# Window attention and a SoLU layer on one core: where two of four loads stand, what a load is planned at, and two transposes set apart

## The chip, the core and the metric

The kernel runs on one core of one Trainium2 chip. The metric is device time in microseconds of one execution. The core's engines are TensorE (PE in the profile; PEld is its weight load), VectorE (DVE), ScalarE (ACT) and GpSimd (POOL); SyncE (SP) issues the DMAs and computes nothing. Each engine works through its own instructions in the order in which the program holds them and waits for the others by semaphores.

## The reference

Eight batches of eight heads attend over 576 positions, each position to itself and the 63 before it; the result is a 4608 x 512 matrix, which goes through a layer with a SoLU activation and a layer norm.

```
scores = where(0 <= rel < 64, q @ k.T / 8, -1e9)
attn   = softmax(scores);  x = attn @ v             # to 4608 x 512
h      = x @ w_in                                   # 512 -> 1024
solu   = h * softmax(h)
ln     = (solu - mean) / sqrt(var + 1e-6) * g_ln
out    = ln @ w_out                                 # 1024 -> 512
```

## The kernel before, in words

**Tiles.** The 4608 tokens are 36 tiles of 128. For each tile the stages are, with the lines of the profile:

- *load* (L338, L343): one DMA brings the tile's queries and keys (qk, 640 KB), one its values (v, 512 KB). Each has a ring of three buffers.
- *scores* (L373, PE), *softmax*: mask and maximum on VectorE (L388), exponential on ScalarE (L393), sums and reciprocals on VectorE (L406, L409), then eight scalings by the reciprocal, one for each head, on GpSimd (L411).
- *cross*: from tile 5 on the softmax tile is turned by DMA. ScalarE copies it, as two halves of 16-bit planes, into a buffer called raw (L425), and SyncE issues one DMA transpose for each half (L428).
- *transposes*: VectorE copies the turned planes into PT (L435). Tiles before the fifth are turned on PE (L446) and copied by ScalarE or VectorE (L451).
- *values* (L470, PE), whose result is split by ScalarE (L484) and VectorE (L485) into a high part xH and a low part xL.
- *moe_in* (L513): 24 matmuls of 512 columns, in three passes (high by high, high by low, low by high), into the only buffer pH. The first three tiles do it in plain fp32 (L502).
- *moe_norm*: maximum on VectorE (L528), exponential on ScalarE (L530), the product with h on VectorE (L533), which is the last to read pH; the sum of squares on ScalarE (L539), small steps for the factor kk on VectorE (L536 to L547) with a power on GpSimd between them (L546), and on GpSimd two halves of the final scaling of e (L550).
- *moe_cross*: VectorE copies each half of e to planes (L576) and SyncE issues a DMA transpose for each (L579); *moe_join* copies the turned planes back into y (VectorE, L589) and splits them (ScalarE L593, VectorE L595). The last two tiles are turned on PE instead, in *moe_transpose* (L610), where ScalarE takes the high part (L619) and VectorE the low one (L621); tiles 0 to 2 go that way as well (L615 for the first two).
- *moe_out* (L646): 24 matmuls, then a copy (ScalarE, L653) and a store (SyncE, L654).

**Order.** At tile t the program runs moe_in of t, the normalisation of t, and moe_out of t - 2. From tile 6 on the attention work is done in pairs: `group(t)`, at every second tile, holds the values of t+1 and t+2, the scores of t+3 and t+4, the loads, and the softmax and cross of t+3 and t+4.

The program doesn't issue instructions directly. It builds a list (`Plan`): each entry has an engine, a cost in nanoseconds, what it reads and writes, and a delay until others may use the result. PE keeps the order of the list. For the others a planner runs the list as in a timetable, by those costs: among the entries of an engine that could begin it takes the one that is due first, counted back from PE's order. SyncE's entries are in the order of the list for the first tiles; those marked loose (loads, stores and transposes of tiles after the third) may be placed freely. A DMA's cost is its size divided by 340 bytes per nanosecond, at least 350 ns. So a change of a cost or of a place in the list can move instructions on SP, DVE, ACT and POOL, and none on PE.

Tensors in the planned orders have the tile's number behind their name (e_18, qk_27). In raw the buffers count 8 for the weights, then 2t + 8 for tile t's softmax planes and 2t + 9 for its planes of the MoE part: raw_54 is the softmax of tile 23, raw_51 the MoE part of tile 21.

Of the kernel before, what the change touches and what calls it, by code (L numbers as in the profile page):

```python
# [18 lines left out]
P = 128  # L19
# [7 lines left out]
AHEAD = 3  # L27
# [15 lines left out]
PAIRS = 6  # L43

SPL = 3

# [8 lines left out]
class Plan:  # L57
# [12 lines left out]
        self.ops.append((engine, cost, emit, reads, writes, lat + self.LATENCY, loose))  # L70

    def dma(self, size, emit, reads, writes, loose=False):
        self.op("SP", max(350, size // 340), emit, reads, writes, 2600, loose)

    def edges(self):

# [91 lines left out]
def tile_window_attention_solu_moe(  # L168
# [17 lines left out]
    nc = tc.nc  # L186

    NT, DM = out.shape
# [6 lines left out]
    NF = DFF // P  # L195
    NTILE = NT // P
    NW = NC + NF // 2
# [23 lines left out]
    for first in (0, None, 1):  # L221
        t = masks[first] = const.tile([P, P], F32, name=f"mask{first}")
# [11 lines left out]
    plan = Plan(RINGS)  # L234

    def T(tag, n, shape, dtype=F32, pool=None):

        if (tag, n) not in plan.tiles:
            plan.tiles[tag, n] = (pool or sb).tile(
                shape, dtype, tag=tag, name=f"{tag}_{n}", bufs=RINGS[tag])  # L240
        return plan.tiles[tag, n]
# [8 lines left out]
    def W32(i):  # L250
        return T("w", i, [P, 2, 512])

    def WL(i):
        return T("w", NW + i, [P, 2, 512], F32R)

    def WH(i, x):
        if i < NC:
            return w_inH[:, i, x * 512:(x + 1) * 512]
        return w_outH[:, 2 * (i - NC) + x]
# [63 lines left out]
    def QK(t):  # L323
        return T("qk", t, [P, NPAIR * (2 * P + WIN)])
# [7 lines left out]
    def V(t, half):  # L332
        return T("v", t, [P, 2, DM])[:, half]

    def load(t, parts=range(2)):

        if 0 in parts:
            plan.dma(P * P * 40, lambda: nc.sync.dma_start(QK(t), qk[t]), [], [("qk", t)],  # L338
                     t > SPL)


        if 1 in parts:
            plan.dma(P * P * 32, lambda: nc.sync.dma_start(  # L343
                T("v", t, [P, 2, DM]).rearrange("p a n -> p (a n)"), v[t]), [], [("v", t)], t > SPL)

    def SS(t):
        return T("sS", t, [P, H, P])
# [7 lines left out]
    def PE_T(t, x):  # L355
        return PS(NTILE + t)[:, x]
# [61 lines left out]
    def XP(t):  # L418
        return T("raw", NW + 2 * t, [P, 4, 2, 512], U16)

    def cross(t):
        if t < CROSS_P:
            return
        for x in range(2):
            plan.op("ACT", 1050, lambda x=x: nc.scalar.copy(  # L425
                XP(t)[:, x], SS(t)[:, 4 * x:4 * x + 4].bitcast(U16).rearrange("p h (n w) -> p w (h n)", w=2)),
                [("sS", t, 4 * x + i) for i in range(4)], [("raw", NW + 2 * t, x)])
            plan.op("SP", 1250, lambda x=x: nc.sync.dma_start_transpose(  # L428
                XP(t)[:, 2 + x].rearrange("p w (h n) -> p (w h) n", h=4), XP(t)[:, x].rearrange("p w n -> p (w n)")),
                [("raw", NW + 2 * t, x)], [("raw", NW + 2 * t, 2 + x)], 2600, t > SPL)  # L430

# [61 lines left out]
    def E(t):  # L493
        return T("e", t, [P, DFF])
# [59 lines left out]
    def YH(t):  # L554
        return T("yH", t, [P, NF, P], F32 if t < PLAIN_OUT else F32R)

    def YL(t):
        return T("yL", t, [P, NF, P], F32R)

    def crosses(t):  # L560
        return CROSS_FROM <= t < NTILE - CROSS_END
# [4 lines left out]
    def EP(t, h):  # L566
        return XB(t)[:, h]

    def TP(t, h):
        return XB(t)[:, 2 + h].rearrange("p w (f n) -> p w f n", f=4)  # L570

    def moe_cross(t):
        if not crosses(t):
            return
        for h in range(2):
# [4 lines left out]
                TP(t, h).rearrange("p w f n -> p (w f) n"), EP(t, h).rearrange("p w n -> p (w n)")),  # L580
                [("raw", NW + 2 * t + 1, h)], [("raw", NW + 2 * t + 1, 2 + h)], 2600, t > SPL)

    def moe_join(t):
        def Y(h):
            return T("y", t, [P, NF, P])[:, 4 * h:4 * h + 4]

        for h in range(2):
            hs = slice(4 * h, 4 * h + 4)
            plan.op("DVE", 740, lambda h=h: nc.vector.tensor_copy(  # L589
                Y(h).bitcast(U16).rearrange("p f (n w) -> p f w n", w=2),  # L590
                TP(t, h).rearrange("p w f n -> p f w n")),
                [("raw", NW + 2 * t + 1, 2 + h)], [("y", t, h)])
            plan.op("ACT", 620, lambda h=h, hs=hs: nc.scalar.copy(YH(t)[:, hs], Y(h)),  # L593
                    [("y", t, h)], [("yH", t, h)])
            plan.op("DVE", 620, lambda h=h, hs=hs: nc.vector.tensor_sub(  # L595
                YL(t)[:, hs], Y(h), YH(t)[:, hs].bitcast(F32)),
                [("y", t, h), ("yH", t, h)], [("yL", t, h)])

    def moe_transpose(t):
        if crosses(t):  # L600
            moe_join(t)
            return
        for h in range(2):
            def pT(h=h):
                return PE_T(t, h)

            def emit(h=h, pT=pT):
                for f in range(4):
                    c = 4 * h + f
                    nc.tensor.transpose(pT()[:, f], E(t)[:, c * P:(c + 1) * P], ident)  # L610

            hs = slice(4 * h, 4 * h + 4)
            plan.op("PE", 430, emit, [("e", t, h)], [("pS", NTILE + t, h)])
            if t < PLAIN_OUT:
                plan.op("DVE", 620, lambda hs=hs, pT=pT: nc.vector.tensor_tensor(  # L615
                    YH(t)[:, hs], pT(), g_sb[:, hs].unsqueeze(2).to_broadcast([P, 4, P]), op=ALU.mult),
                    [("pS", NTILE + t, h), ("g",)], [("yH", t, h)])
                continue
            plan.op("ACT", 560, lambda hs=hs, pT=pT: nc.scalar.copy(YH(t)[:, hs], pT()),  # L619
                    [("pS", NTILE + t, h)], [("yH", t, h)])  # L620
            plan.op("DVE", 620, lambda hs=hs, pT=pT: nc.vector.tensor_sub(  # L621
                YL(t)[:, hs], pT(), YH(t)[:, hs].bitcast(F32)),
                [("pS", NTILE + t, h), ("yH", t, h)], [("yL", t, h)])

    def moe_out(t, middle=None):

        tag = ("pO", t)

        def PO():
            return T(*tag, [P, DM], pool=ps_o)  # L630

        if t < PLAIN_OUT:
            for f in range(NF):
                plan.op("PE", 860, lambda f=f: nc.tensor.matmul(  # L634
                    PO(), YH(t)[:, f], W32(NC + f // 2)[:, f % 2],
                    start=(f == 0), stop=(f == NF - 1)),
                    [("yH", t, f // 4), ("w", NC + f // 2), ("w", NC + f // 2, f % 2)], [tag])
        for f in range(NF if t >= PLAIN_OUT else 0):
            if f == NF // 2 and middle is not None:
                moe_transpose(middle)  # L640
            i, x = NC + f // 2, f % 2
            for k, (y, w, keys) in enumerate((
                    (YH, lambda i, x: WH(i, x), [("yH", t, f // 4), ("H", i, x)]),
                    (YH, lambda i, x: WL(i)[:, x], [("yH", t, f // 4), ("w", NW + i, x)]),
                    (YL, lambda i, x: WH(i, x), [("yL", t, f // 4), ("H", i, x)]))):
                plan.op("PE", 233, lambda f=f, i=i, x=x, k=k, y=y, w=w: nc.tensor.matmul(  # L646
                    PO(), y(t)[:, f], w(i, x), start=(f == k == 0), stop=(f == NF - 1 and k == 2)),
                    keys, [tag])

        def ot():  # L650
            return T("ot", t, [P, DM])

        plan.op("ACT", 580, lambda: nc.scalar.copy(ot(), PO()), [tag], [("ot", t)])  # L653
        plan.dma(P * DM * 4, lambda: nc.sync.dma_start(out[t * P:(t + 1) * P, :], ot()), [("ot", t)], [],  # L654
                 t > SPL)

    def on(f, t, *args):
        if 0 <= t < NTILE:
            f(t, *args)


    def attend(t):
        on(scores, t + AHEAD)
        on(softmax, t + AHEAD)
        on(cross, t + AHEAD)

    load(0, range(1))
    prep(0)
    scores(0)
    softmax(0)  # L670
    load(0, range(1, 2))
    prep(1)
    prep(2)
    load(1)
    transposes(0)
    values(0)
# [10 lines left out]
    def group(t):  # L687
        on(values, t + 1)
        if t != PAIRS:
            on(values, t + 2)  # L690
        both = t + AHEAD, t + AHEAD + 1
        for u in both:
            on(scores, u)
        for u in (t + AHEAD + 2, t + AHEAD + 3):
            on(load, u, range(1))
        for u in (t + AHEAD + 1, t + AHEAD + 2):
            if u != PAIRS + AHEAD + 2:
                on(load, u, range(1, 2))
        for u in both:
            on(softmax, u)  # L700
            on(cross, u)

    for t in range(NTILE + BEHIND):
        if t < PAIRS:
# [17 lines left out]
        else:  # L722
# [22 lines left out]

            last = NTILE - 1 <= t < NTILE + BEHIND - 1
            on(moe_out, t - BEHIND, *([t - BEHIND + 1] if last else []))

    order = plan.order()
# [46 lines left out]
```

## Time and profile before

| | us |
| --- | --- |
| three runs of the kernel | 535.96, 534.41, 532.65 (median 534.41) |
| the profiled execution | 536.71 |
| its span in the trace | 534.9 |

| busy in the span | us | share |
| --- | --- | --- |
| PE, matmuls | 508.7 | 95% |
| PEld, weight loads | 394.4 | 74% |
| DVE | 419.2 | 78% |
| ACT | 357.2 | 67% |
| POOL | 221.6 | 41% |

The profile is of one execution. Busy times are sums over instructions; an engine that is idle is mostly waiting for another, and only what PE waits for can lengthen the execution directly. A wait is put down to the semaphore that came last. The chain of waits is followed back from the last instruction. The granted clock is TensorE's: 1.00 is full speed.

### The profile page before, as it was taken

Reading aid. Unit: us, or ns where it says so; the run is one execution under the profiler, and the core shown is the slowest. Engines: PE = TensorE matmul, PEld = TensorE weight load, DVE = VectorE, ACT = ScalarE, POOL = GpSimd, SP = SyncE. Lnnn points to the kernel's source line nnn. Section 1 sums busy time; section 2 is a strip of 40 time slices with the busy share of each in tenths; the row PEclk is TensorE's granted clock in tenths of the full one; section 3 lists DMA queues with packets and bytes.
Section 4 is the critical chain, followed back from the end, with each engine's and each line's share of the span. In section 5 each row is a group of like instructions: output and inputs, shape, how many; then the busy total and the mean of one; then the engine's idle time right before and its main releaser. Section 6 shows DMA issues by size and latency. Waiting matters only on the chain.

```text
span 534.9 us, 11673 instructions
## 1 busy us (share of the span) xinstructions
PE 508.7 (95%) x4072; PEld 394.4 (74%) x4072; DVE 419.2 (78%) x1327; ACT 357.2 (67%) x959; POOL 221.6 (41%) x406
## 2 busy tenths in 40 slices
PE   2779999999999999999999999979999999999996
PEld 2345576778888887787878787868887888788775
DVE  4979997988787978797979697778777879698630
ACT  4587866679677767677768677684857694956331
POOL 2046067243616461626362526272617161615220
PEclk9989999999999999999999999999999999999999
DMA  8994225789978887777888887967778878457301
GB/s 321 410 387 142 88 74 88 197 191 233 179 217 158 220 155 218 157 217 159 217 158 217 158 217 157 213 132 199 165 156 204 157 215 174 91 104 111 80 21 40
DMA packets 148508, 93.58 MB, mean 175 GB/s; under 512 B 132960, under 2 KB 132960, under 8 KB 148064
## 3 DMA queue, kind: packets, MB, share of 16 engines
q1 hardware_dynamic: 148448, 92.83, 71.0%
q8 instruction: 32, 0.52, 0.4%
q14 instruction: 28, 0.23, 0.1%
HBM read 50.86 MB, written 9.44 MB: 113 GB/s over the span
## 4 chain that ended last, share of the span: by engine, by line
PE 65%; DVE 11%; POOL 8%; DMA 8%; ACT 5%; issue 2%; ACTq 0%; POOLq 0%; DVEq 0%
PE pO L646 26%; PE pH L513 24%; DMA raw<-raw 7%; POOL sS L411 6%; PE pO L470 4%; PE pS L373 4%; PE pH L502 4%; POOL e L550 2%; ACT sS L393 2%; DVE sS L388 1%; DVE raw L576 1%; PE pO L634 1%; DVE PT L435 1%; DVE mst L528 1%; DVE y L589 1%
## 5 line engine op out<-in xcount | busy, mean ns | idle before, releaser
L411 POOL TENSOR_SCALAR sS<-sS,rec 128x128 f32<-128x128 f32 x280 | 122.0, 456 | 49.6 <-DVE nmx L388 26.7
L393 ACT ACTIVATE sS<-sS,nmx 128x128 f32<-128x128 f32 x288 | 111.8, 391 | 10.4 <-DVE nmx L388 9.9
L546 POOL TENSOR_TENSOR mst<-mst,neghalf 128x1 f32<-128x1 f32 x36 | 30.2, 840 | 203.7 <-DVE mst L544 203.7
L646 PE MATMUL pO<-w_outH,yH 128*128 128x512 f32 x272 | 110.1, 405 | 1.2 <-DVE xL L485 1.1
L513 PE MATMUL pH<-w_inH,xH 128*128 128x512 f32 x264 | 106.8, 405 | 3.5 <-DVE mst L533 3.0
L646 PE MATMUL pO<-w,yH 128*128 128x512 f32 x272 | 108.1, 398 | 0.0
L646 PE MATMUL pO<-w_outH,yL 128*128 128x512 f32 x272 | 106.9, 393 | 0.1
L513 PE MATMUL pH<-w,xH 128*128 128x512 f32 x264 | 104.9, 401 | 0.0
L513 PE MATMUL pH<-w_inH,xL 128*128 128x512 f32 x264 | 104.1, 394 | 0.0
L550 POOL TENSOR_SCALAR e<-e,mst 128x512 f32<-128x512 f32 x72 | 66.4, 928 | 45.1 <-DVE mst L547 20.4
L425 ACT COPY raw<-sS 128x1024 uint16<-128x1024 uint16 x62 | 64.3, 1045 | 30.7 <-POOL sS L411 30.6
L589 DVE COPY y<-raw 128x1024 uint16<-128x1024 uint16 x62 | 48.7, 785 | 24.0 <-DMA raw<-raw 23.9
L539 ACT ACTIVATE sq<-e,mst 128x1024 bf16<-128x1024 f32 x36 | 41.4, 1149 | 36.3 <-DVE mst L536 25.0
L513 PEld LDWEIGHTS pH<-w_inH,xH 128*128 128x128 f32 x264 | 49.9, 189 | 18.8 <-issue 3.2
L646 PEld LDWEIGHTS pO<-w_outH,yH 128*128 128x128 f32 x272 | 51.0, 187 | 16.6 <-DVE xL L485 2.4
L576 DVE COPY raw<-e 128x1024 uint16<-128x1024 uint16 x62 | 47.7, 775 | 17.2 <-POOL e L550 17.2
L646 PEld LDWEIGHTS pO<-w_outH,yL 128*128 128x128 f32 x272 | 51.1, 188 | 13.2 <-DVE yL L621 0.5
L513 PEld LDWEIGHTS pH<-w_inH,xL 128*128 128x128 f32 x264 | 50.1, 190 | 12.7 <-issue 0.2
L646 PEld LDWEIGHTS pO<-w,yH 128*128 128x128 f32 x272 | 51.1, 188 | 10.9
L513 PEld LDWEIGHTS pH<-w,xH 128*128 128x128 f32 x264 | 49.9, 189 | 11.4 <-issue 0.2
L388 DVE CUSTOM_DVE_ANT_0 sS<-pS,maskNone 128x128 f32<-128x128 f32 x224 | 53.0, 283 | 4.2 <-PE pS L373 4.2
L593 ACT CAST yH<-y 128x512 fp32r<-128x512 f32 x62 | 38.1, 616 | 26.8 <-DVE y L589 12.5
(66 smaller groups left out, 751.5 us busy)
## 6 DMA issues: line engine op xcount, KB each, us to landing
qk<-qk SPq DMA_DIRECT2D x36, 640.0 KB, 5.6
v<-vS SPq DMA_DIRECT2D x36, 512.0 KB, 4.8
y<-ot SPq DMA_DIRECT2D x36, 256.0 KB, 2.5
raw<-w_out SPq DMA_DIRECT2D x4, 1024.0 KB, 10.8
raw<-w_in SPq DMA_DIRECT2D x3, 1024.0 KB, 11.5
raw<-raw SPq DMA_TRANSPOSE x124, 3.3
raw<-w_in SPq DMA_DIRECT2D x2, 512.0 KB, 6.3
g_sb<-gT SPq DMA_DIRECT2D x1, 4.0 KB, 14.4
```

Source lines behind the costliest of these rows:

```text
L388: plan.op("DVE", 215, lambda h=h: nc.vector.tensor_tensor_reduce(SS(t)[:, h], PS(t)[:, h % 2, h // 2], mk, scale=-SCALE, scalar=BIG, op0=A ...
L393: plan.op("ACT", 390, lambda h=h: nc.scalar.activation(SS(t)[:, h], SS(t)[:, h], AF.Exp, bias=cols("nmx", h), scale=-1.0, accum_out=cols(" ...
L411: plan.op(engine, cost, lambda h=h: v.tensor_scalar(SS(t)[:, h], SS(t)[:, h], rec()[:, h:h + 1], 0.0, ALU.mult, ALU.add), [R], [("sS", t, h)])
L425: plan.op("ACT", 1050, lambda x=x: nc.scalar.copy(XP(t)[:, x], SS(t)[:, 4 * x:4 * x + 4].bitcast(U16).rearrange("p h (n w) -> p w (h n)", ...
L513: plan.op("PE", 233, lambda n=n, c=c, x=x, w=w: nc.tensor.matmul(PH(t)[:, hs], x(t)[:, c], WH(c, h) if w is WH else WL(c)[:, h], start=(n ...
L539: plan.op("ACT", 1200, lambda: nc.scalar.activation(T("sq", t, [P, DFF], BF16), E(t), AF.Square, bias=nmean(), scale=1.0, accum_out=ss()), ...
L546: plan.op("POOL", 560, lambda: nc.gpsimd.tensor_tensor(kk(), kk(), neghalf, op=ALU.pow), [], [key(5)])
L550: plan.op("POOL", 770, lambda h=h, hs=hs: nc.gpsimd.tensor_scalar(E(t)[:, hs], E(t)[:, hs], nmean(), kk(), ALU.add, ALU.mult), [key(4), ke ...
L576: plan.op("DVE", 740, lambda h=h: nc.vector.tensor_copy(EP(t, h), E(t)[:, h * 512:(h + 1) * 512].bitcast(U16).rearrange("p (n w) -> p w n" ...
L589: plan.op("DVE", 740, lambda h=h: nc.vector.tensor_copy(Y(h).bitcast(U16).rearrange("p f (n w) -> p f w n", w=2), TP(t, h).rearrange("p w ...
L593: plan.op("ACT", 620, lambda h=h, hs=hs: nc.scalar.copy(YH(t)[:, hs], Y(h)), [("y", t, h)], [("yH", t, h)])
L646: plan.op("PE", 233, lambda f=f, i=i, x=x, k=k, y=y, w=w: nc.tensor.matmul(PO(), y(t)[:, f], w(i, x), start=(f == k == 0), stop=(f == NF - ...
```

## The change

The planner now takes the loose loads and stores at 240 bytes per nanosecond instead of 340. This is a number of the planner alone; on the chip the transfers have the same size and form. In `group`, the qk load of the even tile (t+6) and the v load of t+4 stay where they were; the qk load of the odd tile (t+7) and the v load of t+5 are listed after softmax and cross and read a key, "gate", which the two plane copies of tile t+4 write. So they are planned behind these copies. The key stands for no data: the loads get no semaphore from it, only their place in SyncE's order. Third, in the two last moe_outs, which hold the transposes of the next tile in their middle, the second half of these transposes comes two rows of w_out, that is six matmuls, later than the first.

```diff
@@ Plan.dma
-        self.op("SP", max(350, size // 340), emit, reads, writes, 2600, loose)
+        self.op("SP", max(350, size // (RATE if loose else 340)), emit, reads, writes, 2600, loose)
@@ load(t, parts=range(2), after=())   # both DMAs: reads [] becomes list(after)
@@ cross
-                [("sS", t, 4 * x + i) for i in range(4)], [("raw", NW + 2 * t, x)])
+                [("sS", t, 4 * x + i) for i in range(4)], [("raw", NW + 2 * t, x), ("gate", t)])
@@ moe_transpose(t, halves=range(2))
-        for h in range(2):
+        for h in halves:
@@ moe_out
-            if f == NF // 2 and middle is not None:
-                moe_transpose(middle)
+            if f in (NF // 2, NF // 4 * 3) and middle is not None:
+                moe_transpose(middle, (f // 2 % 2,))
@@ group
-        for u in (t + AHEAD + 2, t + AHEAD + 3):
-            on(load, u, range(1))
-        for u in (t + AHEAD + 1, t + AHEAD + 2):
-            if u != PAIRS + AHEAD + 2:
-                on(load, u, range(1, 2))
+        if t == PAIRS:
+            on(load, t + AHEAD + 2, range(1))
+        on(load, t + AHEAD + 3, range(1))
+        on(load, t + AHEAD + 1, range(1, 2))
         for u in both:
             on(softmax, u)
             on(cross, u)
+        on(load, t + AHEAD + 4, range(1), [("gate", t + AHEAD + 1)])
+        if t != PAIRS:
+            on(load, t + AHEAD + 2, range(1, 2), [("gate", t + AHEAD + 1)])
```

RATE is 240 and AHEAD is 3. In the changed file the lines stand one or two further down. The instructions are the same in number and kind; on PE only the last transposes move. Three places, each before and then after:

SyncE, from the loads of tiles 26 to 29 to the transposes of tile 22's MoE planes, first before:

```order
L343 DMA v_26_3930<-vS 128x1024
L343 DMA v_27_3956<-vS 128x1024
L338 DMA qk_28_3990<-qk 128x1280
L579 DMA_TRANSPOSE raw_51_3994<-raw_51_3994 128x8x128 x2
L338 DMA qk_29_4035<-qk 128x1280
L579 DMA_TRANSPOSE raw_53_4087<-raw_53_4087 128x8x128 x2
```

Three loads precede the transposes of tile 21 (raw_51), and a fourth those of tile 22. Now SyncE has, from tile 24's softmax planes (raw_56) on:

```order
L430 DMA_TRANSPOSE raw_56_3824<-raw_56_3824 128x8x128 x2
L344 DMA v_25_3865<-vS 128x1024
L656 DMA y<-ot_19_3854 128x512
L339 DMA qk_27_3890<-qk 128x1280
L344 DMA v_26_3940<-vS 128x1024
L581 DMA_TRANSPOSE raw_51_3936<-raw_51_3936 128x8x128 x2
L339 DMA qk_28_4012<-qk 128x1280
L581 DMA_TRANSPOSE raw_53_4084<-raw_53_4084 128x8x128 x2
```

The odd tiles' v and qk have moved up behind the softmax planes, into the group before, on either side of a store; v_26 alone still stands just ahead of raw_51, and qk_28 between the two pairs. All later groups look alike.

GpSimd, from the power of tile 18 (L546) to the scalings of tile 19's e, first before:

```order
L546 TENSOR_TENSOR mst_18_3262<-mst_18_3262,neghalf_100 128x1
L550 TENSOR_SCALAR e_18_3288<-e_18_3288,mst_18_3262 128x512
L411 TENSOR_SCALAR sS_21_3322<-sS_21_3322,rec_21_3428 128x128 x8
L411 TENSOR_SCALAR sS_22_3376<-sS_22_3376,rec_22_3457 128x128 x8
L550 TENSOR_SCALAR e_18_3288<-e_18_3288,mst_18_3262 128x512
L546 TENSOR_TENSOR mst_19_3471<-mst_19_3471,neghalf_100 128x1
L550 TENSOR_SCALAR e_19_3485<-e_19_3485,mst_19_3471 128x512 x2
```

The sixteen softmax scalings of tiles 21 and 22 stand between the two halves of tile 18's e. Now:

```order
L548 TENSOR_TENSOR mst_18_3262<-mst_18_3262,neghalf_100 128x1
L552 TENSOR_SCALAR e_18_3286<-e_18_3286,mst_18_3262 128x512 x2
L413 TENSOR_SCALAR sS_21_3321<-sS_21_3321,rec_21_3425 128x128 x8
L413 TENSOR_SCALAR sS_22_3367<-sS_22_3367,rec_22_3454 128x128 x8
L548 TENSOR_TENSOR mst_19_3468<-mst_19_3468,neghalf_100 128x1
L552 TENSOR_SCALAR e_19_3485<-e_19_3485,mst_19_3468 128x512 x2
```

Both halves precede the sixteen. The same holds now for tiles 10, 16, 18 and so on to 30; before it held for tiles 16 and 22 alone of those with softmax scalings behind them, and tile 26 had eight scalings between its halves.

VectorE in the start, around the first reduction of tile 2 (mst_2), with the copy of tile 3's PT and the low part of a weight (w_8), first before:

```order
L312 TENSOR_TENSOR w_8_588<-w_0_145,w_inH_97 128x512
L451 COPY PT_3_547<-pS_75_539 128x512
L615 TENSOR_TENSOR yH_0_602<-pS_36_591,g_sb_99 128x512
L528 TENSOR_REDUCE mst_2_621<-pH_2_550 128x1
L293 SCALAR_TENSOR_TENSOR w_7_534<-raw_7_422,w_7_534 128x1024
```

Now:

```order
L292 TENSOR_SCALAR w_7_552<-w_7_552 128x1024
L296 SCALAR_TENSOR_TENSOR w_6_458<-raw_6_399,w_6_458 128x1024
L530 TENSOR_REDUCE mst_2_587<-pH_2_550 128x1
L453 COPY PT_3_548<-pS_75_536 128x512
L617 TENSOR_TENSOR yH_0_604<-pS_36_589,g_sb_99 128x512
L294 SCALAR_TENSOR_TENSOR w_7_552<-raw_7_451,w_7_552 128x1024
```

The reduction has moved ahead of the copy of PT_3 and of tile 0's yH.

More of the change, by code (lines that the diff above doesn't have):

```diff
@@ L45 @@
 SPL = 3
+RATE = 240
 RINGS = {
@@ L333, in V, with load @@
         return T("v", t, [P, 2, DM])[:, half]
-    def load(t, parts=range(2)):
+    def load(t, parts=range(2), after=()):
         if 0 in parts:
-            plan.dma(P * P * 40, lambda: nc.sync.dma_start(QK(t), qk[t]), [], [("qk", t)],
+            plan.dma(P * P * 40, lambda: nc.sync.dma_start(QK(t), qk[t]), list(after), [("qk", t)],
                      t > SPL)
@@ L343, in load @@
             plan.dma(P * P * 32, lambda: nc.sync.dma_start(
-                T("v", t, [P, 2, DM]).rearrange("p a n -> p (a n)"), v[t]), [], [("v", t)], t > SPL)
+                T("v", t, [P, 2, DM]).rearrange("p a n -> p (a n)"), v[t]), list(after), [("v", t)],
+                t > SPL)
     def SS(t):
@@ L597, in moe_join, with moe_transpose @@
                 [("y", t, h), ("yH", t, h)], [("yL", t, h)])
-    def moe_transpose(t):
+    def moe_transpose(t, halves=range(2)):
         if crosses(t):
```

## Prediction

> **What bounds the kernel now.** I first read the span, then the busy times by stretch (weights and ramp, 0 to 50; the steady part, 95 to 505; the tail, from 505), to see where TensorE stands idle.
>
> ```profile
> span 534.9 us, 11673 instructions
> 0.00:50.00 50.00, 33.72 (x317) 19.45 (x318) 36.99 (x136) 30.94 (x93) 15.77 (x44) 0.97 0.82 317
> ...
> 95.00:505.00 410.00, 405.01 (x3315) 326.67 (x3314) 333.74 (x1072) 285.03 (x765) 179.83 (x323) 1.00 0.78 176
> 505.00:534.90 29.90, 25.13 (x115) 19.74 (x113) 7.88 (x17) 7.97 (x14) 4.75 (x6) 1.00 0.10 36
> ```
>
> The columns are the stretch, its length, the busy time of PE, PEld, DVE, ACT and POOL, the granted clock, the DMA share and GB/s. PE is busy for 405.01 of 410 us in the steady part, so everything the change could win there is the other 4.99 us, plus whatever a low clock costs. The first stretch has 16.28 us without PE, which belong to weight preparation, and the tail 4.77. The matmuls themselves stay. Next come the waits that end PE's idle time, in the steady part (two rows) and in the tail (one):
>
> ```profile
> PE pH L513 <- DVE mst L533: 3.0, 2, 2.8
> PE pO L646 <- DVE xL L485: 1.1, 2, 0.9
> PE pS L610 <- ACT yH L619: 1.1, 1, 1.1
> ```
>
> One wait of 2.8 us makes most of it: a moe_in that waits until VectorE's product (L533) has read the single pH buffer. The chain of waits shows what was late (start, length, what):
>
> ```profile
> 317.29 5.63 PE pH L513 x24
> ...
> 338.94 0.63 DVE raw L576 x2
> 339.57 6.41 DMA raw<-raw
> ...
> 346.01 0.76 DVE y L589
> 346.77 0.04 DVE mst L547
> ...
> 346.98 2.58 POOL e L550 x2
> 349.55 4.78 POOL sS L411 x8
> ...
> 354.35 0.03 ACT raw L425
> ...
> 355.31 1.21 ACT e L530 x2
> ...
> 356.54 1.23 DVE e L533
> ...
> 357.92 7.36 PE pH L513 x24
> ```
>
> Two DMA transposes of tile 21's normalised planes take 6.41 us. On VectorE the copy of their result (L589) stands ahead of L547, which tile 22's scalings on GpSimd need; behind those stand the softmax scalings, then ScalarE's copies to the planes, behind one of them tile 23's exponential, then its product, then PE. The last row holds a second loss: 24 matmuls took 7.36 us where 24 took 5.63 at 317.29, so 1.73 more. The same columns for the 3.4 us behind the stall show a clock of 0.63 there:
>
> ```profile
> 357.90:361.30 3.40, 3.38 (x10) 2.69 (x11) 3.23 (x10) 3.14 (x6) 0.11 (x1) 0.63 0.67 124
> ```
>
> The stall thus costs 2.78 + 1.73 = 4.51 us.
>
> **The change part by part. Later loads.** SyncE's own sequence at that place, and the landing times of the MoE transposes (minimum, median, maximum) issued in three windows, 338 to 342, 255 to 262 and 421 to 425:
>
> ```profile
> 335.29 1.52 SPq L343 DMA_DIRECT2D v<-vS  x2
> 337.27 0.33 SPq L338 DMA_DIRECT2D qk<-qk  x1
> 339.57 3.87 SPq L579 DMA_TRANSPOSE raw<-raw  x2
> ```
> ```profile
> DMA to landing us min/median/max: 6.4/6.6/6.8
> DMA to landing us min/median/max: 4.3/4.4/4.5
> DMA to landing us min/median/max: 3.5/3.6/3.7
> ```
>
> In the first two windows two v loads and a qk load stand just ahead of the pair; in the third only one v load does. The new order puts one load, the even tile's v, there, and places the odd tile's v and qk behind the four softmax-plane transposes. So I cost the odd tile's MoE transposes as in the third window: 6.6 - 3.6 = 3.0 us earlier at the worst place.
>
> What 3.0 us do to the stall is shown by the place 83 us earlier (tile 17), where GpSimd and VectorE have the same order as at tile 23 but the pair lands in 4.4 us, and by tile 19, where one of the two scalings of the even tile's e stands behind the softmax ones. VectorE's product and PE's next matmul, first of tile 17, then of tile 19; then the stalled one:
>
> ```profile
> 273.40 1.23 DVE L533 CUSTOM_DVE_ANT_0 e<-pH,e 128x1024 f32<-128x1024 f32 x1 [0.23 <-ACT e L530]
> 298.83 1.23 DVE L533 CUSTOM_DVE_ANT_0 e<-pH,e 128x1024 f32<-128x1024 f32 x1 [0.52 <-ACT e L530]
> ```
> ```profile
> 274.78 0.47 PE L513 MATMUL pH<-w_inH,xH 128*128 128x512 f32 x1
> 301.42 0.40 PE L513 MATMUL pH<-w_inH,xH 128*128 128x512 f32 x1
> 357.92 0.47 PE L513 MATMUL pH<-w_inH,xH 128*128 128x512 f32 x1 [2.78 <-DVE mst L533]
> ```
>
> The product ends at 274.63 and PE goes on at 274.78, a stall of about 0.14; at tile 19 it ends at 300.06, 1.36 us before PE is ready. Between tiles 17 and 23 the landing is 2.2 us later and the stall 2.64 larger: nearly one for one. Landing 3.6 instead of 4.4 us after issue would leave about 0.7 us in hand. So the 4.51 us should vanish, and of the other small steady waits (4.99 - 2.78 = 2.21) I take 0.5: **-5.0**. Bounds: -6.7 (4.99 + 1.73) and 0.
>
> The rule in the Trainium skill, "TensorE: Matmul & The Clock Gate", Part 1: The HAM clock gate, is that the clock halves after an idle window of about 3.4 us. By that rule a 2.78 us gap would not itself cause the 1.73, so curing it would leave the 1.73 and the whole sum would be -3.0. The row at 357.90 (0.63) stands right behind this gap of 2.78, so the trace speaks for the gap as the cause, and I go by it.
>
> The deferred loads cost PE nothing if they land in time. They are 5 us transfers whose data are wanted a group later, and a group of two tiles has four blocks of 24 matmuls, 4 x 5.63 = 22.5 us, beside values and scores:
>
> ```profile
> qk<-qk SPq DMA_DIRECT2D x36, 640.0 KB, 5.6
> v<-vS SPq DMA_DIRECT2D x36, 512.0 KB, 4.8
> SPq L343 <- PE pO L470: 58.9, 23, 10.3
> ```
>
> The last row says that SyncE already waited, in order, for the values matmuls to free a v buffer, up to 10.3 us. Behind a v load that waits there stand in the new order the MoE transposes, as before; the softmax-plane ones are now ahead of the odd tile's v. If a load is late after all, values or scores wait and PE with them; without this cover a group would lose up to 5 us.
>
> **GpSimd's order.** Both scalings of an even tile's e now always precede the sixteen softmax scalings; before, one of the two followed them in most groups. One costs the mean of this row:
>
> ```profile
> L550 POOL TENSOR_SCALAR e<-e,mst 128x512 f32<-128x512 f32 x72 | 66.4, 928 | 45.1 <-DVE mst L547 20.4 <-DVE rec L406 15.6 <-ACT sS L393 6.0
> ```
>
> So the softmax planes, and the exponential behind them, come up to 0.93 us later in seven groups or so. The 1.36 of tile 19 covers that with 0.4 left, and tile 17 is the same order with a 4.4 us landing: cost 0, inside the -5.0, as long as the pair lands by about 4.3 us. The VectorE steps for kk now precede the y copies, which helps the same chain; I count nothing for it.
>
> **The tail.** The second half of the last middle transposes waits for ScalarE's read of the first, 1.1 us of PE idle. Rows of the earlier of the two tails and of the later (L619, L610):
>
> ```profile
> 516.06 0.69 DVE L621 TENSOR_TENSOR yL<-pS,yH 128x512 fp32r<-128x512 f32 x1 [1.07 <-ACT yH L619]
> 521.45 0.59 ACT L619 CAST yH<-pS 128x512 fp32r<-128x512 f32 x1 [2.84 <-PE pS L610]
> 522.18 0.63 PE L610 MATMUL pS<-ident,e 128*128 128x128 f32 x4 [1.10 <-ACT yH L619]
> ```
>
> PE would be through the first half at 521.08 (522.18 less 1.10). Six matmuls at 5.63/24 = 0.235 fill 1.4 us, to 522.5. The second half now waits for VectorE's read too: ScalarE is done at 522.04, VectorE 0.69 and a hand-over later, about 522.85. So some 0.4 us remain of 1.1: **-0.7** (bounds -1.1 and +0.4).
>
> **The start.** VectorE's reduction of tile 2 (L528) now stands ahead of the copy of PT_3's second half (L451), which the values of tile 3 need. The row of tile 2's matmuls on PE, then VectorE's:
>
> ```profile
> 49.89 7.10 PE L502 MATMUL pH<-w,xH 128*128 128x512 f32 x16 [0.30 <-DVE mst L533]
> ```
> ```profile
> 57.47 0.69 DVE L451 COPY PT<-pS 128x512 f32<-128x512 f32 x1 [0.22 <-PE pS L446]
> 58.95 1.21 DVE L528 TENSOR_REDUCE mst<-pH 128x1 f32<-128x1024 f32 x1
> ```
>
> The reduction can begin when tile 2's matmuls end, at about 57.0, and ends near 58.2; the copy then ends near 58.9 instead of 58.16, and values(3) starts 0.7 to 0.8 us later. On ScalarE the second PT_2 copy falls behind tile 1's exponential, for another 0.3 at moe_in of tile 2, which mostly waits for GpSimd's scalings anyway. Together **+1.0** (bounds 0 and +2.2, twice the reduction's 1.21 less the 0.22 that VectorE waited there).
>
> **Sum.** -5.0 - 0.7 + 1.0 = -4.7. The profiled execution took 536.71 us (span 534.9 and 1.81 around it), so a like one would take 532.0. It is 2.3 above the median of the runs, 534.41. If those 2.3 lie outside the stalls, the median falls by the full 4.7, to 529.7; if they are part of the big stall, which a shade less contention would shorten, the median goes to 532.0. I take the middle, **531.0**.
>
> **The rivals.** *The transposes come no earlier, or VectorE's order was the stall.* For it: the same three loads preceded a 4.4 and a 6.6 us landing, so the loads alone don't set it. Against it: the one-load window's 3.6. Then only start and tail count, +0.3: 534.7.
>
> *Slower: the adjacent scalings with late transposes.* If pairs go on landing above 4.3 us, the groups that now gain the adjacent order lose their margin: each would stall as tiles 17 and 23 did, 0.14 or 2.78, at the mean 1.46. Seven groups make +10.2, with +0.3 from the ends 10.5: 534.4 + 10.5 = 544.9. For it: the new order is exactly that of the two groups that stalled. Against it: only one of those stalled for long, and its landing was 2.2 us later. It decides where L533 ends after PE has finished its moe_out.
>
> *The full gain.* All 6.72 steady, the tail's 1.1, nothing lost at the start: -7.8, and by the two readings 526.6 or 528.9, say 528. Against it: waits such as L485's belong to no load.
>
> **How the numbers follow.** Forecast 0.55, no earlier transposes 0.24, full gain 0.13, slower 0.08. The likeliest is 531.0. The range runs from 527.5, just under the full gain, to 536.0, above the second case with the upper start bound; it leaves out the slower case and the far edges. About 1%, 5.3 us, is what can be told from no change: below 529.07 is faster, above 539.75 slower. The forecast's spread of some 1.5 us around 531.0 puts a fifth of it under that bound, and the full gain most of its 0.13: 0.22. Slower keeps 0.07, and 0.71 is left.
>
> **What would show it.** Right: no PE wait on L533 above 1 us, no clock under 0.9 in the steady part, MoE transposes of odd tiles landing in about 3.6 us, steady PE idle near 2 us, about 0.4 us at the second last-tile transpose, and values(3) later. Wrong: landings still of 6 us, waits of L513 on L533 in several groups, or PE waiting for v or qk.

## The result

The changed kernel takes 531.09 us (median of 18 runs, 529.28 to 533.49), the kernel before 535.56 (median of 18, 532.1 to 539.36). The ratio is 0.9918, with a 95% interval of 0.9897 to 0.9938: 4.4 us faster, a little under one per cent. The profiled execution has a span of 529.4 us where that of before had 534.9.

Busy time by stretch in the profile after (stretch, its length, PE, PEld, DVE, ACT, POOL, granted clock, DMA share, GB/s):

```profile
0.00:50.00 50.00, 32.67 (x320) 18.94 (x321) 38.52 (x138) 32.46 (x98) 18.66 (x45) 1.00 0.83 319
...
95.00:500.00 405.00, 402.31 (x3308) 324.44 (x3308) 329.16 (x1064) 282.61 (x764) 183.50 (x322) 1.00 0.79 176
```

PE is idle for 405.00 - 402.31 = 2.69 us of the steady part, against 4.99 before. PE's waits there, and in the tail:

```profile
PE pH L515 <- DVE mst L535: 1.6, 4, 0.8
PE pO L472 <- DVE PT L437: 0.8, 2, 0.4
...
PE pS L612 <- DVE mst L539: 0.2, 1, 0.2
PE pS L612 <- DVE yL L623: 0.2, 1, 0.2
```

The 2.8 us wait of moe_in on the product is gone; four small ones are left, 0.8 us at most. The 1.1 us wait in the tail has become two of 0.2. SyncE at the place of the old stall, and the landing of its two MoE transposes (tile 21):

```profile
331.34 0.38 SPq L339 DMA_DIRECT2D qk<-qk  x1
334.87 0.33 SPq L344 DMA_DIRECT2D v<-vS  x1
335.66 3.94 SPq L581 DMA_TRANSPOSE raw<-raw  x2
339.70 0.53 SPq L339 DMA_DIRECT2D qk<-qk  x1
```
```profile
DMA to landing us min/median/max: 4.0/4.6/5.1
```

PE passes the same matmuls in the same order in both kernels up to the tail, so the two traces can be laid beside each other matmul by matmul. At the first three-pass moe_out (matmul 642 of 4072, whose start is at 94.09 us before and 92.49 after) the changed one has gained 1.6 us. From there to matmul 3980, the last before the tail's transposes matter, it gains 3.8 (416.03 against 412.21 us), in the tail 0.7 (20.72 against 19.99), and from the end of the last matmul to the end of the execution it loses 0.6 (3.7 against 4.3). Together that is 5.5.

### The profile page after: what moved, and what is told of

Read it like the earlier page. It is cut to its first block, busy times and chain, and to the rows that moved or that the text cites. A ratio compares the mean times of both kernels' runs of the same rounds, so it can differ in the third digit from the quotient of the medians.

```text
span 529.4 us, 11654 instructions
## 1 busy us (share of the span) xinstructions
PE 504.7 (95%) x4072; PEld 392.2 (74%) x4072; DVE 417.3 (79%) x1327; ACT 356.0 (67%) x959; POOL 224.6 (42%) x406
## 4 chain that ended last, share of the span: by engine, by line
PE 58%; DVE 17%; POOL 8%; DMA 8%; ACT 6%; issue 2%; ACTq 0%; POOLq 0%; DVEq 0%
PE pH L515 23%; PE pO L648 19%; DMA raw<-raw 7%; POOL sS L413 5%; PE pO L472 4%; PE pS L375 4%; PE pH L504 3%; DVE sS L390 3%; PE pO L636 3%; POOL e L552 3%; DVE y L591 3%; DVE e L535 2%; ACT sS L395 2%; DVE raw L578 2%; DVE mst L530 1%
## 5 line engine op out<-in xcount | busy, mean ns | idle before, releaser
L413 POOL TENSOR_SCALAR sS<-sS,rec 128x128 f32<-128x128 f32 x280 | 123.7, 460 | 50.7 <-DVE nmx L390 26.7
L548 POOL TENSOR_TENSOR mst<-mst,neghalf 128x1 f32<-128x1 f32 x36 | 28.2, 784 | 187.6 <-DVE mst L546 187.6
L552 POOL TENSOR_SCALAR e<-e,mst 128x512 f32<-128x512 f32 x72 | 69.5, 972 | 50.9 <-DVE mst L549 23.7
L530 DVE TENSOR_REDUCE mst<-pH 128x1 f32<-128x1024 f32 x36 | 43.8, 1216 | 19.5 <-PE pH L515 18.7
L578 DVE COPY raw<-e 128x1024 uint16<-128x1024 uint16 x62 | 45.2, 732 | 17.5 <-POOL e L552 17.5
L591 DVE COPY y<-raw 128x1024 uint16<-128x1024 uint16 x62 | 48.6, 787 | 10.4 <-DMA raw<-raw 10.3
```

Source lines behind the costliest of these rows:

```text
L413: plan.op(engine, cost, lambda h=h: v.tensor_scalar(SS(t)[:, h], SS(t)[:, h], rec()[:, h:h + 1], 0.0, ALU.mult, ALU.add), [R], [("sS", t, h)])
L530: plan.op("DVE", 1150, lambda: nc.vector.tensor_reduce(nmax(), PH(t), axis=AX.X, op=ALU.max, negate=True), [("pH", t)], [key(0)])
L548: plan.op("POOL", 560, lambda: nc.gpsimd.tensor_tensor(kk(), kk(), neghalf, op=ALU.pow), [], [key(5)])
L552: plan.op("POOL", 770, lambda h=h, hs=hs: nc.gpsimd.tensor_scalar(E(t)[:, hs], E(t)[:, hs], nmean(), kk(), ALU.add, ALU.mult), [key(4), ke ...
L578: plan.op("DVE", 740, lambda h=h: nc.vector.tensor_copy(EP(t, h), E(t)[:, h * 512:(h + 1) * 512].bitcast(U16).rearrange("p (n w) -> p w n" ...
L591: plan.op("DVE", 740, lambda h=h: nc.vector.tensor_copy(Y(h).bitcast(U16).rearrange("p f (n w) -> p f w n", w=2), TP(t, h).rearrange("p w ...
```

## The experiments

**Neither part alone.** The first theories were L, that what counts is which loads stand ahead of the odd tile's MoE transposes in SyncE's queue, and O, that the planner's new order on VectorE, ScalarE and GpSimd makes the gain. First the three parts apart, and the kernel before once more. A ratio is the time over that of the kernel before in the same session, with its 95% interval; in the diffs, longer code is told in words.

*e_load:* loads put off, RATE 340, tail as before.

```diff
-RATE = 240
+RATE = 340
-            if f in (NF // 2, NF // 4 * 3) and middle is not None:
-                moe_transpose(middle, (f // 2 % 2,))
+            if f == NF // 2 and middle is not None:
+                moe_transpose(middle)
```

> Only the two loads of a group are put off; the planner still counts 340 bytes per nanosecond and the tail is as before. If the place of the loads makes the gain (theory L: fewer loads just ahead of the odd tile's MoE transposes), nearly all of the steady part's gain is here: 3 to 4 us faster than before (ratio about 0.993 to 0.995), and the odd tiles' MoE transposes land sooner than the 4.45 us median of before. If the order that the planner happens to find on VectorE and GpSimd makes it (theory O), the result can be anything between -4 and +2 us, as that order differs from both kernels, and it follows when tile t's planes are issued, not how long they take to land.

Measured: ratio 1.0038 (1.0009 to 1.0068), slightly slower than before. Theory L as I had put it missed.

*e_rate:* the kernel before with the planner's number alone.

```diff
-        self.op("SP", max(350, size // 340), emit, reads, writes, 2600, loose)
+        self.op("SP", max(350, size // (240 if loose else 340)), emit, reads, writes, 2600, loose)
```

> Only the planner's 240 bytes per nanosecond; the loads stay ahead of the softmax and the tail is as before. Theory L: no gain (ratio 0.998 to 1.002), since as many loads stand ahead of the transposes. Theory O: a change of either sign, -3 to +3 us, since half of VectorE's order in the steady part is another.

Measured: 1.0008 (0.9984 to 1.0031), no change.

*e_tail:* the kernel before with the last transposes apart.

```diff
-            if f == NF // 2 and middle is not None:
-                moe_transpose(middle)
+            if f in (NF // 2, NF // 4 * 3) and middle is not None:
+                moe_transpose(middle, (f // 2 % 2,))
```

> Only the two transposes set apart. Both theories: the 1.1 us wait of the second half shrinks to 0.2 to 0.4, so 0.7 to 0.9 us faster (ratio about 0.9985), at the edge of what five rounds can tell; in the profile the wait at the second transposes in the tail is 0.4 or less.

Measured: 0.9985 (0.9954 to 1.0016), as expected but not told from no change. From matmul 3980 to the last it takes 20.22 us where before took 20.72; the wait at the second transposes is 0.5 us, a little over the 0.4 expected.

*e_loadrate:* the change without its third part.

```diff
-            if f in (NF // 2, NF // 4 * 3) and middle is not None:
-                moe_transpose(middle, (f // 2 % 2,))
+            if f == NF // 2 and middle is not None:
+                moe_transpose(middle)
```

> The change without the transposes set apart. Both theories: 0.7 us slower than the change, 3.5 us or so faster than before (ratio 0.993), with the 1.1 us wait in the tail back.

Measured: 0.9911 (0.9878 to 0.9945). So the gain is, within what can be told, in the first two parts together, which each give nothing alone.

*b2:* no edit; the kernel before profiled again.

> The kernel before once more, for its profile. If the 2.8 us stall and the half clock behind it belong to the kernel's order, they stand again at about 355 to 358 us. If they are an accident of one execution (a slower landing of two transposes), the stall is under 1 us or elsewhere, and the half clock of 3.4 us near 34 us and near 358 us may be missing.

Measured: 534.3 us in its one run; the stall stands again, a little shorter. PE's row in b2, then the clock behind it and that of a stretch in its start:

```profile
357.26 0.47 PE L513 MATMUL pH<-w_inH,xH 128*128 128x512 f32 x1 [2.20 <-DVE mst L533]
```
```profile
357.20:360.60 3.40, 3.33 (x14) 2.74 (x15) 3.23 (x10) 3.19 (x6) 0.04 (x1) 1.00 0.67 128
```
```profile
24.50:27.90 3.40, 3.40 (x4) 0.90 (x4) 2.30 (x5) 2.50 (x14) 0.00 (x0) 0.50 1.03 412
```

The stall of 2.2 to 2.8 us is the order's (e_tail, with the same order up to the tail, has 2.26 us there); the half clock behind it is not in every execution: here the clock is 1.00 there. Both traces of the kernel have a stretch of 3.4 us of half clock in the start, here at 24.5 us.

**Orders of different kernels joined.** To part L from O I gave SyncE the order of e_loadrate and the other engines that of before (*h_sp*), and the reverse (*h_comp*).

```diff
-        return [self.ops[i][2] for i in out]
+        chains["SP"].sort(key=place of the instruction in the other kernel's SyncE order)
+        out = all five chains and the dependencies, merged
+        return [self.ops[i][2] for i in out]
```

> PE, VectorE, ScalarE and GpSimd keep the order of before, word for word; SyncE alone has the order of the change (its loads later), and the tail is as before. Theory L (the loads' place): the whole steady gain, 3 to 4 us (ratio 0.993 to 0.995), no wait of moe_in on L533 over 1 us. Theory O (the order of the compute engines): no gain (ratio 0.998 to 1.002), and the 2.8 us wait near tile 23 stands.

> The counterpart: SyncE has the order of before, the compute engines that of the change, the tail as before. Theory O: 3 to 4 us faster (ratio 0.993 to 0.995). Theory L: no gain, or, by the slower rival of the prediction (adjacent scalings with late transposes), up to 10 us slower (ratio 1.00 to 1.02).

Measured: 1.0746 (1.0706 to 1.0786) and 1.1299 (1.1265 to 1.1333). Neither theory had this. SyncE works in order, so a transpose whose planes are written later in one order than in the other holds up all behind it. What SyncE waited for on the plane copies (42.1 us in the kernel before), and PE on the product, in h_comp:

```profile
SPq L634 <- DVE raw L631: 97.3, 18, 10.0
```
```profile
PE pH L568 <- DVE mst L588: 55.6, 10, 9.4
```

These two tell L and O apart no more than the first three did; they show that an order for SyncE holds good only with the orders it was planned with.

**Small moves inside one order.** So I moved single instructions in kernels that otherwise keep their order. The rival is now I: the transposes land as late as they are issued late, and in before tile 21's are issued 11.2 us after the start of the moe_in behind (339.57 - 328.38, that matmul's start), in the changed kernel 7.8 (335.66 - 327.88). In the edits, `find` gives the planned instructions of an engine that write a key, and `move` puts them directly ahead of (0) or behind (1) another one; all else keeps its order.

*b_early:* the kernel before, VectorE's order changed in two groups.

```diff
+        for t in (15, 21):
+            kk = [i for i in find("DVE", ("mst", t, 5))][-1:]
+            move("DVE", kk, find("DVE", ("mst", t + 1, 0))[0], 0)
+            planes = [i for h in (0, 1) for i in find("DVE", ("raw", 9 + 2 * t, h))]
+            move("DVE", planes, find("DVE", ("xL", t + 2))[0], 1)
```

> The kernel before with three VectorE instructions moved up in two groups: the last step for kk of tiles 15 and 21, ahead of the next tile's maximum, and the two copies of these tiles' MoE planes, ahead of the next tile's product. SyncE's loads stay. Theory I (when the transposes are issued): issue falls from 11.2 to about 9 us after the start of the moe_in behind, the second landing of tile 21 from 18 to 19 to about 16 to 17, and the stall near 357 us from 2.2 to 2.8 to under 1: 2 to 4 us faster (ratio 0.9925 to 0.9965). Theory L (what stands ahead of them in the queue): nothing, ratio 0.998 to 1.002, as the same three loads stand there.

Measured: 1.0015 (0.9984 to 1.0047). SyncE there, and the landing of the pair:

```profile
339.82 2.02 SPq L383 DMA_DIRECT2D v<-vS  x2
341.94 0.38 SPq L378 DMA_DIRECT2D qk<-qk  x1
342.41 6.56 SPq L619 DMA_TRANSPOSE raw<-raw  x2
```
```profile
DMA to landing us min/median/max: 9.0/9.0/9.0
```

The pair is issued earlier within its group (9.5 us after the moe_in's start) and lands 9.0 us after issue instead of 6.6. All that was won at the issue was lost behind the loads; PE waited 2.78 and 2.85 us behind the products of tiles 17 and 23. (The profiled execution took 540.96 us, one of the longest of the twelve; their median is 536.86.) Theory I fails here.

*b_loads:* the kernel before, SyncE's order alone: loads directly ahead of an odd tile's MoE pair go behind it.

```diff
+        for t in range(9, 30, 2):
+            turns = [i for h in (2, 3) for i in find("SP", ("raw", 9 + 2 * t, h))]
+            loads = the qk and v loads that stand directly ahead of turns[0]
+            move("SP", loads, turns[-1], 1)
```

> The kernel before with only SyncE's order changed, and that only where loads stand directly ahead of an odd tile's two MoE transposes: these loads go directly behind them. Theory L: the transposes land in 3.2 to 3.6 us each instead of 4.3 to 6.8, the stall near 357 us goes, 2.5 to 4.5 us faster (ratio 0.9915 to 0.995). Theory I: issue at 11.2 us as before at tiles 15 and 21, so at most half of that; and if the even tile's transposes or a load come late instead, slower (above 1.002).

Measured: 0.9899 (0.9861 to 0.9937), the full gain of the change with none of its parts. The pair and its landing, and PE's wait there:

```profile
341.57 3.53 SPq L622 DMA_TRANSPOSE raw<-raw  x2
```
```profile
DMA to landing us min/median/max: 4.1/4.4/4.6
```
```profile
PE pH L556 <- DVE mst L576: 0.6, 1, 0.6
```

The issue is as late as before (11.2 us into the group), the landing 2.2 us sooner, the stall 0.6. For the kernel before, that is theory L.

*a_late:* the changed kernel with the plane copies of the odd tiles moved behind the product.

```diff
+        for t in range(17, 30, 2):
+            planes = [i for h in (0, 1) for i in find("DVE", ("raw", 9 + 2 * t, h))]
+            move("DVE", planes, find("DVE", ("mst", t + 1, 2))[0], 1)
```

> The changed kernel with the two plane copies of tiles 17, 19 to 29 moved behind the next tile's product on VectorE; the loads stay as changed. Theory I: issue at 11.2 instead of 7.7 us, second landing at 16.5 to 18.5, a wait of moe_in on the product of 0.5 to 2.5 us in each of the seven groups, 5 to 15 us slower than the change (ratio to before 1.001 to 1.02). Theory L: the loads stand as in the change, so the gain stays (ratio 0.991 to 0.994).

Measured: 1.0069 (1.0041 to 1.0096), 8 us slower than the change. Its waits on the product:

```profile
PE pH L553 <- DVE mst L573: 8.9, 8, 1.9
```

Here theory I holds: with the loads as in the change, a pair issued 11.0 us into the group costs 0.9 to 1.9 us in each of the seven groups, though the transposes land only 3.1 to 4.6 us after issue. So both count: the pair can't land before its own 3 us or more are over, nor before the loads ahead of it.

How late is too late depends on VectorE's order as well. In b_loads and in a_late tile 21's pair is issued equally late and lands in the same 4.1 to 4.6 us, yet PE then waits 0.6 us in the one and 1.85 in the other. The last step for kk and the scalings of tile 22's e behind it, in b_loads and then in a_late:

```profile
346.94 0.04 DVE mst L590
...
347.15 3.60 POOL e L593 x2
```
```profile
350.96 0.08 DVE mst L587
...
351.21 2.37 POOL e L590 x2
```

The first transpose landed at 346.16 and 347.92. In b_loads one copy of y stands between it and this step, as in the kernel before; in a_late, as in the changed kernel, both copies and parts of the softmax mask do. So the scalings start 1.0 us after the landing in the one and 3.3 us in the other. No run moves this step alone.

*a_loads:* the changed kernel with the remaining v load put behind the pair.

```diff
+            loads = the v loads that stand directly ahead of turns[0]
+            move("SP", loads, turns[-1], 1)
```

> The changed kernel with the one v load that still stands directly ahead of an odd tile's MoE transposes moved directly behind them. The landing there falls from about 5 to 3.5 us by both theories; with the issue at 7.7 us there is little left to win: the waits of 0.8, 0.3, 0.2 and 0.15 us go, 0 to 1.5 us faster than the change (ratio to before 0.989 to 0.992). If the v load then comes late, values wait for it and it is slower than the change.

Measured: 0.9867 (0.9826 to 0.9909). The pair of tile 21 lands 3.1 us after issue, but VectorE's copies begin no sooner, since other work stands ahead of them. The interval overlaps that of the change (0.9897 to 0.9938) and the spans are 529.6 and 529.4: not told apart.

**Why the parts fail alone.** In e_load, planned at 340, tile 28's qk stands again between the v load and the pair of tile 21, so three loads precede it, as before:

```profile
336.83 0.38 SPq L339 DMA_DIRECT2D qk<-qk  x1
339.10 0.33 SPq L344 DMA_DIRECT2D v<-vS  x1
341.09 0.33 SPq L339 DMA_DIRECT2D qk<-qk  x1
342.61 4.30 SPq L581 DMA_TRANSPOSE raw<-raw  x2
```
```profile
DMA to landing us min/median/max: 6.2/6.5/6.8
```

*el_qk:* e_load with only this load moved, in the five groups where it stands there.

```diff
+            loads = the qk loads that stand directly ahead of turns[0]
+            move("SP", loads, turns[-1], 1)
```

> The kernel with the loads put off and the planner left at 340 (ratio 1.0038), with one thing changed on SyncE: in the five groups where the even qk load stands directly ahead of an odd tile's two MoE transposes (tiles 9, 13, 17, 21, 25), it goes directly behind them. Theory L: at tile 21 the first landing falls from 6.8 us after its issue to 5 or less, the waits of moe_in on the product after tiles 13, 17 and 21 (1.06, 0.28 and 1.32 us) go or fall under 0.4, and the time falls by 2 to 3 us (ratio 0.997 to 1.000). Theory P (the whole planned order of the compute engines, not this load, holds that kernel back): ratio stays at 1.002 to 1.006 and the waits stay.

Measured: 0.9961 (0.9934 to 0.9989), clear of e_load's 1.0009 to 1.0068. The pair and its landing:

```profile
337.93 0.33 SPq L387 DMA_DIRECT2D v<-vS  x1
341.54 2.97 SPq L624 DMA_TRANSPOSE raw<-raw  x2
```
```profile
DMA to landing us min/median/max: 3.2/3.4/3.7
```

The three waits after tiles 13, 17 and 21 are gone; two of 0.8 and 1.5 us stand earlier, at 195 and 223 us, so it does not reach the change. One load's place is worth 0.8% of the whole kernel: putting off v and qk clears the way only if the planner, at 240 bytes per nanosecond, also thinks the even qk load long enough to go behind the pair. What keeps el_qk 0.4% from the change is somewhere in the rest of the planned order, and no run shows where. For e_rate this was not tried; in its trace a v and a qk load still precede the pair at tile 21, which is issued 11.2 us into the group, and PE waits 1.69 us.

The queue in numbers, at tile 21's pair (landing of the last load and of the first transpose are issue plus landing time in each kernel's trace):

| kernel | last load ahead lands | pair issued | first transpose lands | behind that load | PE waits |
| --- | --- | --- | --- | --- | --- |
| before | 343.5 | 339.57 | 346.0 | 2.5 | 2.78 |
| b_early | 349.0 | 342.41 | 351.4 | 2.4 | 2.85 |
| e_load | 347.1 | 342.61 | 349.4 | 2.4 | 1.32 |
| changed | 339.8 | 335.66 | 340.8 | 1.0 | 0 |
| el_qk | 343.8 | 341.54 | 344.7 | 0.9 | 0 |

In no row does a transpose land ahead of a load that was issued before it, and none of the 124 transposes does in any of the fourteen traces.

## Why the prediction was right, and where its steps failed

The time (531.0 against 531.1) and the direction were right. The mechanism of the largest term was right for the kernel before: the loads ahead of the odd tile's pair set its stall, b_loads shows it alone. For the changed kernel it was half of what happened. Quick landings alone are not enough there: a_late has them (3.1 to 4.6 us) with the issue at 11.0 us into each group, and is 0.7% slower than before. The change also issues the pairs earlier, and for that the sum had no term. Its parts:

- **Later loads: -5.0 forecast, -3.8 in the profiled pair.** The stall and its half clock, 4.51, went as forecast. The step "I cost the odd tile's MoE transposes as in the third window" failed in size: tile 21's land 4.0 to 5.1 us after issue, and those of tiles 17 to 29 4.0 to 6.6, not 3.6. The even v load stands 0.8 us ahead of the pair (334.87 and 335.66); in the third window it stood 2.4 us ahead (420.04 and 422.46). The trace of before held a nearer case, tile 17's pair:

```profile
281.73 0.34 SPq L343 DMA_DIRECT2D v<-vS  x1
282.60 3.88 SPq L579 DMA_TRANSPOSE raw<-raw  x2
```
```profile
DMA to landing us min/median/max: 4.6/4.9/5.2
```

What made up for it was not in the sum: tile 21's pair is issued 3.4 us earlier in the group (7.8 against 11.2), because VectorE's order puts the plane copies ahead of the product. a_late, which issues the pairs of all seven groups at 11.0 us (before, they stood between 6.8 and 11.2), loses 8 us. And the other steady waits did not shrink by 0.5; they grew from 2.21 (4.99 - 2.78) to 2.69. The 3.8 is one draw besides: b2 and e_tail have the order of before up to the tail and take 413.63 and 417.35 us from matmul 642 to 3980, where the profile of before took 416.03; e_loadrate, with the change's order, takes 412.68. From mean to mean that is 3.2 us, from pair to pair 1.0 to 5.1.
- **GpSimd's order: 0 forecast.** Both scalings stand ahead of the sixteen in the changed kernel, and its longest wait on the product is 0.8 us. But the condition set for this, a landing by about 4.3 us, was not met: in the seven groups of tiles 17 to 29 the first transpose of the pair lands 5.0 to 6.6 us after its issue. So the slower rival had its condition and still didn't come, because the pairs are issued earlier. And "the VectorE steps for kk now precede the y copies" is a misreading: the last step (L549) now stands behind both copies of y (L591), where at tile 22 before it stood behind the first alone. In the changed kernel:

```profile
341.31 0.75 DVE L591 COPY y<-raw 128x1024 uint16<-128x1024 uint16 x1
...
342.58 0.75 DVE L591 COPY y<-raw 128x1024 uint16<-128x1024 uint16 x1
...
344.24 0.15 DVE L549 TENSOR_TENSOR mst<-mst 128x1 f32<-128x1 f32 x1
```
- **The rival "the transposes come no earlier, or VectorE's order was the stall"** is half true: the earlier issue is VectorE's order. But an earlier issue alone, behind the old loads, gains nothing (b_early).
- **The tail: -0.7 forecast, -0.7 measured** (20.72 to 19.99 us). The waits were 0.2 and 0.2, where 0.4 at one place was forecast.
- **The start: +1.0 forecast, -1.6 measured, and neither is the order's.** VectorE and PE after:

```profile
55.76 1.23 DVE L530 TENSOR_REDUCE mst<-pH 128x1 f32<-128x1024 f32 x1 [0.17 <-PE pH L504]
56.90 0.68 DVE L453 COPY PT<-pS 128x512 f32<-128x512 f32 x1
```
```profile
48.59 7.13 PE L504 MATMUL pH<-w,xH 128*128 128x512 f32 x16 [0.28 <-DVE mst L535]
...
56.96 1.36 PE L472 MATMUL pO<-PT,v 128*64 128x64 f32 x32
```

The copy does stand behind the reduction, until 57.58, but values(3) begins at 56.96: the step failed in that PE takes the heads of PT's other half first. Its 32 matmuls take 1.36 us instead of 1.15, so 0.2 is what the copy costs. The 1.6 us come from the clock. From 34 to 38 us it was 0.57 in the profile of before and 1.00 after (rows in this order):

```profile
34.00:38.00 4.00, 3.45 (x34) 2.48 (x35) 2.54 (x16) 4.00 (x13) 2.46 (x8) 0.57 1.02 410
```
```profile
34.00:38.00 4.00, 3.58 (x38) 2.14 (x39) 3.41 (x17) 4.00 (x12) 2.58 (x6) 1.00 1.03 413
```

Executions alike in this are alike at matmul 642: e_tail has the old start and no slow stretch there, 92.44 us, the changed kernel 92.49; b2 and e_loadrate both have one, 94.06 and 94.08. So the start's order costs next to nothing, and the 1.6 is an accident of the executions: a_loads, with the changed start, has no slow stretch there either, and a_late, with the same start, has one.
- **From the execution to the median.** The middle of two readings was taken. With 18 runs the median of before is 535.56, so the profiled execution stands 1.15 above it and not 2.3, and the median fell by 4.5, nearly the full sum of 4.7: the first reading was the nearer. The 531.0 stood for a fall of 3.4 from 534.41. That median was 1.15 too low and the fall 1.1 too small, so that the time came out to a tenth is luck. Nor is the gain mainly a matter of the half clock: the changed kernel's eight executions with a granted clock of 0.999 or more average 530.4 us, nineteen such of the kernel before, from the later sessions, 534.8. The medians of before in those sessions are 0.4 to 1.6 us above 535.56, so some 3 to 4 us of gain remain at full clock.

So the sum's size was right in part by errors that cancel: the steady part gave 1.2 less than forecast, and the start's order cost about 1.0 less.

## What to carry to other kernels

Look at what a small, urgent DMA stands behind in its queue, not only at when it can be issued: here, large loads whose data no matmul needed for another 26 us (the pair issued at 339.57, the next values at 365.21) stood ahead of transposes on the critical path, and moving only them (b_loads) gave as much as the whole change. A cost in a planner can matter more by the one place where it tips the order than by its size, so compare the orders, and test a part on its own before crediting it. One profile's stalls include accidents of the clock; profile the same kernel twice before counting a start-up difference.

## What the runs showed of the hardware

DMA transposes issued from SyncE's queue land behind loads issued earlier from the same queue, 0.9 to 2.5 us after the last of them (the table above). Issued 1.7 us earlier behind the same three loads (b_early), they landed no earlier. At tile 21, with the last load 3.6 us ahead, they took 3.2 to 3.7 us (el_qk), with loads put directly behind them 3.1 (a_loads) and 4.1 to 4.6 us (b_loads).

TensorE's clock falls after shorter gaps than I had thought, and not after each. The stretch behind a 2.26 us gap in e_tail, and two stretches of h_sp around the matmul that follows a 1.39 us gap:

```profile
357.60:361.00 3.40, 3.40 (x8) 2.72 (x9) 3.23 (x10) 3.11 (x6) 0.16 (x1) 0.51 0.71 133
```
```profile
137.50:141.50 4.00, 3.92 (x25) 3.12 (x26) 3.31 (x21) 3.27 (x18) 2.25 (x4) 0.65 0.25 93
138.70:142.10 3.40, 3.40 (x9) 2.61 (x9) 2.71 (x14) 2.07 (x12) 2.73 (x6) 0.50 0.00 1
```

A gap of 2.78 us (before, b_early) was followed by half clock each time, one of 2.26 too, one of 2.20 (b2) and one of 1.85 (a_late) not, one of 2.20 and one of 1.39 in h_sp again. "TensorE: Matmul & The Clock Gate" in the Trainium skill, Part 1: The HAM clock gate, names an idle window of about 3.4 us. The slow stretches here are 3.4 us long or a multiple of it, but a full 3.4 us of idle time was not needed.

The granted clock in the traces changes only on a grid of 3.41 us, whose phase differs from execution to execution. Cut along this grid from 15 us on, the fourteen traces have 14 pieces at full clock in which PE is busy for less than 45% of the time, and each is followed by a piece at half clock; 2040 with more than 57%, none of them followed by one; and 37 between, of which 11 are. The pieces that hold the gaps of 2.78 (before), 2.20 (b2), 2.26 (e_tail) and 1.39 us (h_sp), with PE busy for 25, 52, 36 and 56%:

```profile
355.37:358.78 3.41, 0.86 (x4) 0.76 (x5) 2.24 (x4) 3.41 (x6) 1.75 (x6) 1.00 0.83 186
355.62:359.03 3.41, 1.76 (x8) 1.49 (x9) 3.15 (x7) 3.41 (x7) 0.82 (x3) 1.00 0.68 143
354.12:357.53 3.41, 1.21 (x6) 0.63 (x4) 1.32 (x3) 3.41 (x5) 2.65 (x8) 1.00 0.98 217
135.26:138.67 3.41, 1.90 (x35) 1.56 (x35) 3.41 (x15) 2.01 (x9) 0.09 (x1) 1.00 0.66 237
```

So what parts equal gaps here is how much of a gap falls into one piece of the grid, with both outcomes near one half. This is a count over traces, not an experiment. It fits the start too, where e_loadrate's piece ahead of its slow stretch has PE busy for 51%.
